# Elementwise work of GpSimd moved to VectorE in the opening of a three-stage kernel (one core)

## The chip, the cores and the metric

The kernel runs on one core of one Trainium2 chip. The metric is device time in microseconds (us) of one execution. A core has TensorE (PE in the profile, with its weight loads as PEld), VectorE (DVE), ScalarE (ACT), GpSimd (POOL) and SyncE (SP, which here only issues DMAs). Each engine works through its own queue in order and waits on semaphores of the others.

## The reference, cut to what matters

Three layers follow each other. The first is gated linear attention over 4 batches, 8 heads, 768 positions and head size 48; the second a dense layer with the Mish activation; the third a top-1 mixture of eight experts.

```
for t in range(S):                                  # attention
    state = alpha[t][:, None] * state + outer(k[t], v[t])
    y[t] = q[t] @ state
h = x @ w_in;  g = h * tanh(softplus(h));  x2 = g @ w_out          # 3072 x 384 -> 2048 -> 384
expert = argmax(x2 @ w_gate);  out = gate * relu(x2 @ w1[expert]) @ w2[expert]
```

## The kernel before, in words

Tokens go in 8 tiles of 384; a tile is 3 attention units of 128 positions of one batch (24 units, all 8 heads in each). A tile takes 16 steps, one for each 128 columns of the hidden layer. A step is `mm1` (9 matmuls, L622), the activation (`act_tanh` for each step, `act_mish` for three steps at once) and, six steps later, `mm2` (9 matmuls, L680). After the 16th `mm2` of a tile, `route` picks the expert. Matrices are split into a high half, which ScalarE writes by rounding, and a low half, the difference: three products stand for one full one.

Before the steady loop over tiles there is an opening, whose order is a string of short tokens: attention of units 0 to 5 (`a_prep1`, `a_prep2`, `a_kt`, `a_qk`, `a_y`, `a_kv`), the unpacking of 16 weight blocks (`prep_w`, then `prep_c` for the gate's columns), and the steps 0 to 15 of the first tile as their weights arrive. The compiler's scheduler puts each engine's instructions in order by its own estimate of when each is ready, so the order in a queue is not that of the string.

What the change touches:

- `prep_w(f)`: ScalarE makes the exponent part (L61), VectorE assembles the words in four instructions (L62, L63, L66, L69), ScalarE writes the high halves of w_in and w_out (L408), GpSimd the two low halves (L409). Two blocks of words (`wbits`) and two raw blocks (`wraw`) are held; the next raw block's DMA waits for L69.
- `a_prep1(u)`: two scans on VectorE (L437, L451) of alpha against reset rows `rst1`, `rst2`, with small instructions between (L444, L447, L448).
- `a_prep2(u)`: products of k (L463, GpSimd) and q (L464, VectorE for units 0 to 2, else GpSimd) with the scans.
- `a_qk(u)`: the masked scores. For units 0 to 5 ScalarE copies them out of PSUM (L506) and GpSimd masks them (L507); for later units VectorE does both in one instruction (L512).
- `act_mish(s)`: VectorE multiplies (L665), ScalarE rounds to the high half (L666), GpSimd subtracts for the low half `gl` (L668).

Of the kernel before, what the change touches and what calls it, by code (L numbers as in the profile page):

```python
# [7 lines left out]
F32 = mybir.dt.float32  # L8
# [4 lines left out]
AF = mybir.ActivationFunctionType  # L13
ALU = mybir.AluOpType
# [4 lines left out]
P = 128  # L19
B, H, S, D = 4, 8, 768, 48  # L20
NP = H // 2
NCH = S // P
NU = B * NCH
NT, DM = B * S, H * D
DFF = 2048
NF = DFF // P
# [5 lines left out]
NTILE = NT // TT  # L32
G = TT // P
# [23 lines left out]
def w_bits(nc, t, raw):  # L57
    words = raw.bitcast(I32).rearrange("p (n t) -> p n t", t=2)
    hi, lo = words[:, :, 1], words[:, :, 0]
    tf = t.bitcast(F32)  # L60
    nc.scalar.activation(out=tf, in_=hi.bitcast(F32), func=AF.Abs)  # L61
    nc.vector.tensor_scalar(out=tf, in0=tf, scalar1=MINW, scalar2=None, op0=ALU.max)  # L62
    nc.vector.tensor_scalar(  # L63
        out=t, in0=t, scalar1=3, scalar2=0x3FFFFFFF, op0=ALU.logical_shift_left, op1=ALU.bitwise_and
    )
    nc.vector.scalar_tensor_tensor(  # L66
        out=t, in0=hi, scalar=-0x40000000, in1=t, op0=ALU.bitwise_and, op1=ALU.bitwise_or
    )
    nc.vector.scalar_tensor_tensor(  # L69
        out=t, in0=lo, scalar=29, in1=t, op0=ALU.logical_shift_right, op1=ALU.bitwise_or  # L70
    )
# [203 lines left out]
def kernel(ctx: ExitStack, tc: tile.TileContext, att, w_io, w_gate, w1, w2, out):  # L275
    nc = tc.nc
    root = ctx.enter_context(ExitStack())

    const = root.enter_context(tc.tile_pool(name="const", bufs=1))
# [26 lines left out]
    def wt_f(f):  # L306
        return [t[:, f % (NF // 2)] for t in wt[f // (NF // 2)]]
# [13 lines left out]
    def bank(u, name):  # L321
        if u < G:
            nps[0] += 1
            k = nps[0] % 5
            if k < 2:
                return ps_a.tile([P, 512], F32, tag="att", name=name)
            return ps_acc.tile([P, 512], F32, tag=f"acc{k - 2}", name=name)
        return ps_a.tile([P, 512], F32, tag="att", name=name)
# [12 lines left out]
    def load_w(f):  # L341
        if f < NF:
            wraw[f] = s0p.tile([P, 2 * DM], I64, tag="wraw", name="wraw", bufs=2)
            nc.sync.dma_start(out=wraw[f], in_=w_io[f])
# [6 lines left out]
    load_unit(2)  # L351
    load_w(1)

    ident = const.tile([P, P], F32, name="ident")
    nc.gpsimd.memset(ident, 1.0)
    nc.gpsimd.affine_select(
        out=ident, in_=ident, pattern=[[-1, P]], compare_op=ALU.is_equal, fill=0.0, base=0, channel_multiplier=1
    )
    mask = const.tile([P, P], F32, name="mask")
    nc.gpsimd.memset(mask, 1.0)  # L360
    nc.gpsimd.affine_select(
        out=mask, in_=mask, pattern=[[1, P]], compare_op=ALU.is_ge, fill=0.0, base=0, channel_multiplier=-1
# [4 lines left out]
        out=before, in_=before, pattern=[[1, P]], compare_op=ALU.is_gt, fill=0.0, base=0, channel_multiplier=-1  # L367
# [12 lines left out]
    for e in range(E):  # L380
        nc.gpsimd.memset(ecap[:, e:e + 1], e * ROOM / P)
        nc.gpsimd.memset(full[:, :, e:e + 1], float((e + 1) * ROOM))
        nc.gpsimd.memset(desc[:, :, e:e + 1], float(E - e))
    rst1 = const.tile([P, NP, P + 1], F32, name="rst1")
    rst2 = const.tile([P, NP, P + 1], F32, name="rst2")
    nc.gpsimd.memset(rst1, 0.0)
    nc.gpsimd.memset(rst1[:, :, 0:1], 1.0)
    nc.gpsimd.memset(rst2, 0.0)
    chk = const.tile([P, NTILE * G * E + NU * NP], F32, name="chk")
    chk_l = chk[:, 0:NTILE * G * E].rearrange("p (j g e) -> p j g e", g=G, e=E)  # L390
    chk_a = chk[:, NTILE * G * E:].rearrange("p (u a o) -> p u a o", a=NP, o=1)
# [8 lines left out]
    def prep_w(f):  # L400
        raw = wraw.pop(f)
        t = s0p.tile([P, 2 * DM], I32, tag="wbits", name="wbits", bufs=2)
        tf = t.bitcast(F32)
        w_bits(nc, t, raw)
        ih, il, oh, ol = wt_f(f)
        ih, il = (x.rearrange("p k m -> p (k m)") for x in (ih, il))
        for h, l, x in ((ih, il, tf[:, 0:DM]), (oh, ol, tf[:, DM:])):
            nc.scalar.activation(out=h[:, 0:DM], in_=x, func=AF.Copy)  # L408
            nc.gpsimd.tensor_tensor(out=l[:, 0:DM], in0=x, in1=h[:, 0:DM].bitcast(F32), op=ALU.subtract)  # L409
        load_w(f + 2)  # L410
        wb[f] = tf

# [43 lines left out]
    def a_prep2(u):  # L456
        if u >= NU:
            return
        t = unit_t[u]
        sc1, sc2 = st[u]  # L460
        q3 = t[:, OQ:OK].rearrange("p (a b) -> p a b", b=P)
        k3 = t[:, OK:OV].rearrange("p (a b) -> p a b", b=P)
        nc.gpsimd.tensor_tensor(out=k3, in0=k3, in1=sc1[:, :, 1:], op=ALU.mult)  # L463
        (nc.vector if u < G else nc.gpsimd).tensor_tensor(out=q3, in0=q3, in1=sc2[:, :, 1:], op=ALU.mult)  # L464
        st[u] = [sc1, k3, q3]

    state = {}
# [21 lines left out]
    def a_qk(u):  # L489
        sc1, kc, qc, kn, am = st[u]  # L490
        both = [bank(u, "qk").rearrange("p (a b) -> p a b", b=P) for _ in range(2)]
        last = None
        for a in range(NP):
            for i in (1, 0):
                r = slice(64 * i, 64 * i + 64)
                mm = nc.tensor.matmul(both[i][:, a], kc[r, a], qc[r, a], start=True, stop=True)
                if last is not None:
                    tc.add_manual_dep(
                        mm.ins, last.ins.name,
                        mybir.DependencyInfo(mybir.DependencyClass.NoSync, mybir.DependencyReason.DATA),  # L500
                        reason="heads in turn"
                    )
                last = mm
        for i in (1, 0):
            if u < 2 * G:
                nc.scalar.activation(out=am[:, :, i], in_=both[i], func=AF.Copy)  # L506
                nc.gpsimd.affine_select(  # L507
                    out=am[:, :, i], in_=am[:, :, i], pattern=[[0, NP], [1, P]], compare_op=ALU.is_ge, fill=0.0,
                    base=0, channel_multiplier=-1
                )  # L510
            else:
                nc.vector.tensor_tensor(  # L512
                    out=am[:, :, i], in0=both[i], in1=mask.unsqueeze(1).to_broadcast([P, NP, P]), op=ALU.mult
                )

    def a_y(u):
        sc1, kc, qc, kn, am = st[u]
# [47 lines left out]
    def att_phase(u, k):  # L565
        if u >= NU:
            return
        if k == 0:
            a_kt(u)
        elif k == 1:  # L570
            a_qk(u)
            a_prep1(u + 1)
        elif k == 2:
            pass
        elif k == 3:
            a_y(u)
            a_prep2(u + 1)
        else:
            a_kv(u)
            load_unit(u + 2)  # L580
# [47 lines left out]
    def after_act(inst):  # L628
        for x in inst:
            if seq:  # L630
                tc.add_manual_dep(
                    x.ins, seq[0].ins.name,
                    mybir.DependencyInfo(mybir.DependencyClass.NoSync, mybir.DependencyReason.DATA), reason="tables"
                )
            seq[:] = [x]
# [15 lines left out]
    def act_mish(s):  # L651
        b, i = divmod(s, KB)
        if i < KB - 1 and s < NTILE * NF - 1:
            return
        h, t = batch.pop(b)
        tf = t[:, 0:i + 1].rearrange("p k t -> p (k t)")
        after_act([
            nc.scalar.activation(out=tf, in_=tf, func=AF.Arctan, scale=-0.5, bias=half),
            nc.scalar.preload_act_table_set("silu_and_others"),
            nc.scalar.activation(out=tf, in_=tf, func=AF.Sin, scale=-2.0, bias=quart),  # L660
        ])
        for x in range(i + 1):
            gh = s2p.tile([P, TT], F32R, tag="gh", name="gh", bufs=KB)
            gl = s2p.tile([P, TT], F32R, tag="gl", name="gl", bufs=KB)
            nc.vector.tensor_tensor(out=t[:, x], in0=t[:, x], in1=h[:, x], op=ALU.mult)  # L665
            nc.scalar.activation(out=gh, in_=t[:, x], func=AF.Copy)  # L666
            eng = nc.vector if s == NTILE * NF - 1 else nc.gpsimd
            eng.tensor_tensor(out=gl, in0=t[:, x], in1=gh.bitcast(F32), op=ALU.subtract)  # L668
            live[s - i + x] = (gh, gl)

# [14 lines left out]
    fill = []  # L685
# [78 lines left out]
    def step(s):  # L764
        if s < nsteps:
            mm1(s)
            act_tanh(s)
            act_mish(s)
        d = s - LAG
        if d >= 0:  # L770
            mm2(d)
            if d % NF == NF - 1:
                return route(d // NF)
# [10 lines left out]
    def more_w(_):  # L784
# [3 lines left out]
    nsteps = NTILE * NF  # L788
    does = {
        "a": a_prep1, "b": a_prep2, "t": a_kt, "q": a_qk, "y": a_y,  # L790
        "v": a_kv, "l": load_unit, "w": prep_w, "c": prep_c, "h": warm, "m": step, "z": zero, "P": more_w
    }
    warm(12)
# [8 lines left out]
    for s in range(NF, nsteps + LAG):  # L802
# [17 lines left out]
        out=flb, in0=fl[:, 0:1], scalar1=0.0, scalar2=0.0, op0=ALU.is_le, op1=ALU.is_equal  # L820
# [11 lines left out]
        out=flag, in0=fl[:, 1:2], scalar=float(CAP), in1=fl[:, 2:3], op0=ALU.is_gt, op1=ALU.add  # L832
# [218 lines left out]
```

## Time and profile before

| what | value |
| --- | --- |
| time, median of 3 runs | 901.82 us (900.13 to 905.32) |
| profiled execution, its own time | 900.5 us |
| its span in the profile | 898.8 us |
| busy: PE, DVE, ACT, POOL | 827.8, 501.4, 525.3, 321.8 us |
| mean granted TensorE clock | 0.957 |

The span is what lies between the first and the last instruction; 1.7 us of the execution lie outside it. Busy time is a union of intervals, waits for a busy port included; a line of the `lines` view adds the idle time of the engine just before the group, and what ended it.

### The profile page before, as it was taken

What the parts mean: (1) busy time and instruction counts of PE and PEld (TensorE: products, weight loads), DVE (VectorE), ACT (ScalarE), POOL (GpSimd) and SP (SyncE); (2) the same over time, 40 slices, a digit from 0 to 9 for tenths busy, and PEclk for the clock granted to TensorE, in tenths of its full rate; (3) what the DMA queues carried; (4) which work ended last, traced back from release to release, by engine and by line L of the source; (5) the groups of instructions that cost most, each with busy time, mean ns of one, the idle gap of its engine ahead of it and who ended that gap; (6) DMA issues with size and microseconds to landing.
All of it is one profiled execution on the core that took longest, in us unless ns stands there. A gap on an engine that the chain in (4) does not pass through costs nothing. (4 is left out here: it accounts for less than half of the span.)

```text
span 898.8 us, 15088 instructions
## 1 busy us (share of the span) xinstructions
PE 827.8 (92%) x5988; PEld 761.1 (85%) x5988; DVE 501.4 (56%) x952; ACT 525.3 (58%) x826; POOL 321.8 (36%) x359
## 2 busy tenths in 40 slices
PE   7778785999999999999999999996699999999994
PEld 4667675889999999999999989896699999999994
DVE  7986876476465676566566554734443553354220
ACT  3365665657776677766776667884443653455221
POOL 5674754254344444354354342243001011100111
PEclk9787797999999999999999999999799999999998
DMA  6733342721022012112121101300733543453001
GB/s 245 237 106 118 106 133 100 207 80 65 29 86 76 15 69 91 40 48 83 45 77 48 49 27 48 95 28 19 238 120 126 177 150 106 147 182 116 26 30 34
DMA packets 22012, 85.86 MB, mean 96 GB/s; under 512 B 3232, under 2 KB 9012, under 8 KB 18988
## 3 DMA queue, kind: packets, MB, share of 16 engines
q1 hardware_dynamic: 18348, 75.31, 25.7%
q0 software_dynamic: 3584, 9.50, 3.0%
q8 instruction: 49, 0.80, 0.4%
q14 instruction: 31, 0.25, 0.1%
HBM read 68.35 MB, written 17.03 MB: 95 GB/s over the span
## 5 line engine op out<-in xcount | busy, mean ns | idle before, releaser
L668 POOL TENSOR_TENSOR gl<-tau,gh 128x384 fp32r<-128x384 f32 x126 | 135.0, 1081 | 171.7 <-ACT gh L666 116.8
L622 PE MATMUL h<-xh,wi_h 128*128 128x384 f32 x384 | 138.0, 360 | 8.7 <-ACT wi_h L408 6.1
L622 PE MATMUL h<-xh,wi_l 128*128 128x384 f32 x384 | 134.2, 350 | 5.1 <-POOL wi_l L409 5.0
L680 PE MATMUL acc<-wo_h,gh 128*128 128x392 f32 x384 | 133.4, 348 | 1.6 <-ACT gh L666 1.0
L622 PE MATMUL h<-xl,wi_h 128*128 128x384 f32 x384 | 133.3, 347 | 0.0
L680 PE MATMUL acc<-wo_l,gh 128*128 128x392 f32 x384 | 132.4, 345 | 0.0
L665 DVE TENSOR_TENSOR tau<-tau,hc 128x384 f32<-128x384 f32 x128 | 81.6, 690 | 86.1 <-ACT tau L660 46.0
L680 PE MATMUL acc<-wo_h,gl 128*128 128x392 f32 x384 | 126.5, 346 | 1.5 <-POOL gl L668 1.5
L888 PE MATMUL g<-eh,ew 128*128 128x432 f32 x384 | 118.6, 363 | 0.0
L648 ACT ACTIVATE tau<-h 128x384 f32<-128x384 f32 x128 | 60.7, 490 | 91.5 <-PE h L622 64.4
L902 POOL DMA_INDIRECT out_dram<-yo,xg x32 | 31.7, 991 | 228.8 <-ACT yo L901 214.2
L933 PE MATMUL y<-hh,ew 128*128 128x432 f32 x336 | 105.5, 365 | 1.4 <-ACT hh L892 1.4
L893 DVE SCALAR_TENSOR_TENSOR hl<-g,hh 128x432 fp32r<-128x432 f32 x64 | 38.5, 603 | 91.4 <-ACT hh L892 91.4
L666 ACT ACTIVATE gh<-tau 128x384 fp32r<-128x384 f32 x128 | 66.0, 523 | 37.7 <-PE acc L680 19.3
L622 PEld LDWEIGHTS h<-xh,wi_h 128*128 128x128 f32 x384 | 74.2, 194 | 15.5 <-ACT wi_h L408 8.2
L609 DVE TENSOR_TENSOR ew<-est,ew 128x512 fp32r<-128x512 f32 x96 | 64.2, 718 | 34.7 <-ACT ew L608 33.3
L892 ACT ACTIVATE hh<-g 128x432 fp32r<-128x432 f32 x64 | 33.4, 524 | 82.4 <-PE g L888 82.0
L622 PEld LDWEIGHTS h<-xh,wi_l 128*128 128x128 f32 x384 | 74.6, 194 | 8.1 <-POOL wi_l L409 7.2
L649 DVE COPY hc<-h 128x384 f32<-128x384 f32 x128 | 67.9, 545 | 19.1 <-ACT tau L648 19.1
L680 PEld LDWEIGHTS acc<-wo_h,gh 128*128 128x128 f32 x384 | 73.4, 191 | 3.5 <-ACT gh L666 2.2
L888 PEld LDWEIGHTS g<-eh,ew 128*128 128x128 f32 x384 | 72.7, 190 | 3.4
L622 PEld LDWEIGHTS h<-xl,wi_h 128*128 128x128 f32 x384 | 74.4, 194 | 1.1 <-issue 0.6
(141 smaller groups left out, 1621.7 us busy)
## 6 DMA issues: line engine op xcount, KB each, us to landing
unit<-in_att_dram SPq DMA_DIRECT2D x23, 1026.5 KB
est<-in_w_dram SPq DMA_DIRECT2D x28, 768.0 KB
wraw<-in_w_io_dram SPq DMA_DIRECT2D x16, 768.0 KB
xs<-zrow SPq DMA_DIRECT2D x3, 1746.0 KB
xg<-xs SPq DMA_DIRECT2D x7, 654.8 KB
est<-in_w_dram SPq DMA_DIRECT2D x4, 512.0 KB
xs<-zrow SPq DMA_DIRECT2D x1, 1552.0 KB
est<-in_w_dram SPq DMA_DIRECT2D x4, 256.0 KB
```

The costliest lines, as they stand in the source:

```text
L609: nc.vector.tensor_tensor(out=tl[:, cs], in0=tx, in1=th[:, cs].bitcast(F32), op=ALU.subtract)
L622: nc.tensor.matmul(ps, l[:, k], r[:, k], start=(n == 0), stop=(n == 3 * KC - 1))
L648: nc.scalar.activation(out=t[:, i], in_=hbuf[s], func=AF.Tanh, scale=0.5)
L649: nc.vector.tensor_copy(out=h[:, i], in_=hbuf.pop(s))
L665: nc.vector.tensor_tensor(out=t[:, x], in0=t[:, x], in1=h[:, x], op=ALU.mult)
L666: nc.scalar.activation(out=gh, in_=t[:, x], func=AF.Copy)
L668: eng.tensor_tensor(out=gl, in0=t[:, x], in1=gh.bitcast(F32), op=ALU.subtract)
L680: nc.tensor.matmul(acc[j][g][:, 0:DM + E], l[:, gs], w, start=(f == 0 and i == 0), stop=(f == NF - 1 and i == 2))
L888: nc.tensor.matmul(ps, l[:, k, fs], r[:, k], start=(n == 0), stop=(n == 3 * KC - 1))
L892: nc.scalar.activation(out=hh, in_=ps, func=AF.Relu)
L893: nc.vector.scalar_tensor_tensor(out=hl, in0=ps, scalar=0.0, in1=hh.bitcast(F32), op0=ALU.max, op1=ALU.subtract)
L933: nc.tensor.matmul(yac[e][c], l[:, f, cs], r, start=(f == 0 and i == 0), stop=(f == NF2 - 1 and i == 2))
```

## The change

Four kinds of GpSimd work go to VectorE, and the reset rows are set before the other constants. The low halves of all 16 weight blocks, the k and q products of units 0 to 5, the low halves of the steps that are activated before step 16 (`s < NF`, five batches of three) and the masks of units 0 to 5 are VectorE's; the masks read PSUM directly, and ScalarE's copy in front of them goes. Left on GpSimd are the constants, the check L441, the state product L484, and the products of units from 6 on.

```diff
@@ (constants)
+    rst1 = const.tile([P, NP, P + 1], F32, name="rst1")
+    rst2 = const.tile([P, NP, P + 1], F32, name="rst2")
+    nc.gpsimd.memset(rst1, 0.0)
+    nc.gpsimd.memset(rst1[:, :, 0:1], 1.0)
+    nc.gpsimd.memset(rst2, 0.0)
     ident = const.tile([P, P], F32, name="ident")
...
-    (the same five lines, behind the other constants)
@@ prep_w
-            nc.gpsimd.tensor_tensor(out=l[:, 0:DM], in0=x, in1=h[:, 0:DM].bitcast(F32), op=ALU.subtract)
+            nc.vector.tensor_tensor(out=l[:, 0:DM], in0=x, in1=h[:, 0:DM].bitcast(F32), op=ALU.subtract)
@@ a_prep2
-        nc.gpsimd.tensor_tensor(out=k3, in0=k3, in1=sc1[:, :, 1:], op=ALU.mult)
-        (nc.vector if u < G else nc.gpsimd).tensor_tensor(out=q3, in0=q3, in1=sc2[:, :, 1:], op=ALU.mult)
+        eng = nc.vector if u < 2 * G else nc.gpsimd
+        eng.tensor_tensor(out=k3, in0=k3, in1=sc1[:, :, 1:], op=ALU.mult)
+        eng.tensor_tensor(out=q3, in0=q3, in1=sc2[:, :, 1:], op=ALU.mult)
@@ a_qk
-            if u < 2 * G:
-                nc.scalar.activation(out=am[:, :, i], in_=both[i], func=AF.Copy)
-                nc.gpsimd.affine_select(out=am[:, :, i], in_=am[:, :, i], ...)
-            else:
-                nc.vector.tensor_tensor(out=am[:, :, i], in0=both[i], in1=mask..., op=ALU.mult)
+            nc.vector.tensor_tensor(out=am[:, :, i], in0=both[i], in1=mask..., op=ALU.mult)
@@ act_mish
-            eng = nc.vector if s == NTILE * NF - 1 else nc.gpsimd
+            eng = nc.vector if s < NF or s == NTILE * NF - 1 else nc.gpsimd
```

## Rows read from the trace of the kernel before

**Rows 1.** Busy time by stretch: span, PE, PEld, DVE, ACT, POOL, clock, DMA.
```profile
0.00:165.00 165.00, 126.33 (x916) 106.66 (x917) 122.06 (x162) 87.49 (x157) 95.09 (x124) 0.82 0.46 154
165.00:190.00 25.00, 23.70 (x212) 21.58 (x211) 16.90 (x48) 18.91 (x28) 8.12 (x10) 1.00 0.49 151
10.00:60.00 50.00, 38.35 (x328) 31.27 (x328) 45.34 (x60) 25.96 (x49) 34.62 (x31) 0.80 0.54 180
```

**Rows 2.** Waits of PE, 0 to 165 us: total, times, longest.
```profile
PE wc L423 <- ACT wot L420: 11.8, 5, 4.3
...
PE h L622 <- POOL wi_l L409: 5.0, 5, 2.7
...
PE y L534 <- POOL am L507: 1.0, 1, 1.0
```

**Rows 3.** Groups of POOL by line, 0 to 172 us: busy, mean ns, idle before.
```profile
L409 POOL TENSOR_TENSOR wo_l<-wbits,wo_h 128x384 fp32r<-128x384 f32 x16 | 22.9, 1429 | 0.0
L668 POOL TENSOR_TENSOR gl<-tau,gh 128x384 fp32r<-128x384 f32 x16 | 20.9, 1325 | 9.5 <-ACT gh L666 7.0 <-issue 2.5
L409 POOL TENSOR_TENSOR wi_l<-wbits,wi_h 128x384 fp32r<-128x384 f32 x16 | 19.3, 1206 | 40.3 <-ACT wi_h L408 37.5 <-PE wt L418 2.9
L463 POOL TENSOR_TENSOR unit<-unit,sc 128x512 f32<-128x512 f32 x8 | 10.8, 1355 | 0.6
L507 POOL TENSOR_SCALAR_AFFINE_SELECT am<-am 128x512 f32<-128x512 f32 x12 | 9.0, 765 | 1.2 <-ACT am L506 1.2
```

**Rows 4.** Groups of DVE by line, 0 to 172 us.
```profile
L66 DVE SCALAR_TENSOR_TENSOR wbits<-wraw,wbits 128x768 int32<-128x768 int32 x16 | 19.1, 1195 | 0.3
L69 DVE SCALAR_TENSOR_TENSOR wbits<-wraw,wbits 128x768 int32<-128x768 int32 x16 | 16.9, 1059 | 0.2
L62 DVE TENSOR_SCALAR wbits<-wbits 128x768 f32<-128x768 f32 x16 | 15.3, 956 | 14.0 <-ACT wbits L61 14.0
L63 DVE TENSOR_SCALAR wbits<-wbits 128x768 int32<-128x768 int32 x16 | 14.0, 878 | 0.4
L665 DVE TENSOR_TENSOR tau<-tau,hc 128x384 f32<-128x384 f32 x18 | 13.2, 782 | 5.2 <-ACT tau L660 5.2
...
L448 DVE SCALAR_TENSOR_TENSOR rst<-sc,rc 128x4 f32<-128x4 f32 x8 | 6.9, 865 | 0.2
```

**Rows 5.** Timeline of DVE: start us, us, instruction.
```profile
6.36 1.16 DVE L448 SCALAR_TENSOR_TENSOR rst<-sc,rc 128x4 f32<-128x4 f32 x1
...
34.07 0.15 DVE L448 SCALAR_TENSOR_TENSOR rst<-sc,rc 128x4 f32<-128x4 f32 x1
...
96.95 0.96 DVE L66 SCALAR_TENSOR_TENSOR wbits<-wraw,wbits 128x768 int32<-128x768 int32 x1
...
100.48 0.56 DVE L62 TENSOR_SCALAR wbits<-wbits 128x768 f32<-128x768 f32 x1 [1.00 <-ACT wbits L61]
```

**Rows 6.** Timeline of POOL, same columns.
```profile
4.54 0.10 POOL L387 MEMSET rst<- 128x4 f32 x1
...
6.31 1.19 POOL L463 TENSOR_TENSOR unit<-unit,sc 128x512 f32<-128x512 f32 x1
...
46.63 1.93 POOL L409 TENSOR_TENSOR wo_l<-wbits,wo_h 128x384 fp32r<-128x384 f32 x1
...
104.76 4.70 POOL L668 TENSOR_TENSOR gl<-tau,gh 128x384 fp32r<-128x384 f32 x3
...
155.61 2.91 POOL L668 TENSOR_TENSOR gl<-tau,gh 128x384 fp32r<-128x384 f32 x3
```

**Rows 7.** Line L668 alone, whole span: duration min/median/max in ns.
```profile
L668 POOL TENSOR_TENSOR gl<-tau,gh x126: 988/1020/1729, 54.3 to 615.9; 128x384 fp32r<-128x384 f32 x126
...
L668 DVE TENSOR_TENSOR gl<-tau,gh x2: 544/550/557, 617.3 to 618.0; 128x384 fp32r<-128x384 f32 x2
```

**Rows 8.** Mask of later units on DVE, groups by line, 0 to 260 us.
```profile
L512 DVE TENSOR_TENSOR am<-qk,mask 128x512 f32<-128x512 f32 x8 | 5.2, 679 | 1.3 <-PE qk L496 1.3
```

**Rows 9.** PE's first instructions, timeline, columns as in rows 5.
```profile
1.90 7.69 PE L760 MATMUL warm<-ones 128*128 128x512 bf16 x28 [1.90 <-POOL ones L374]
```

More of the change, by code (lines that the diff above doesn't have):

```diff
@@ L383 @@
         nc.gpsimd.memset(desc[:, :, e:e + 1], float(E - e))
[L384 to L388, printed above, removed]
     chk = const.tile([P, NTILE * G * E + NU * NP], F32, name="chk")
@@ L504, in a_qk @@
         for i in (1, 0):
-            if u < 2 * G:
-                nc.scalar.activation(out=am[:, :, i], in_=both[i], func=AF.Copy)
[L507 to L510, printed above, removed]
-            else:
-                nc.vector.tensor_tensor(
-                    out=am[:, :, i], in0=both[i], in1=mask.unsqueeze(1).to_broadcast([P, NP, P]), op=ALU.mult
-                )
+            nc.vector.tensor_tensor(
+                out=am[:, :, i], in0=both[i], in1=mask.unsqueeze(1).to_broadcast([P, NP, P]), op=ALU.mult
+            )
     def a_y(u):
```

## The prediction

> **What bounds the kernel now.** I first read busy time by stretch. From 0 to 165 us PE works 126.3 of 165 us and its clock is granted at 0.82 on the mean, so it swings between its two levels, 1.2 and 2.4 GHz; from 165 to 190 us it works 23.7 of 25 us at 1.00 [rows 1]. Behind 190 us PE stays the bound, and the change has no instruction there (its units are 0 to 5, its steps those below 16). So everything is decided in the opening: a microsecond by which PE fills up earlier is a microsecond of the whole.
>
> In the opening no engine is full. DVE works 122.1 us, ACT 87.5, POOL 95.1 [rows 1]; DVE's gaps are 42.9 us, and in the densest stretch, 10 to 60 us, it is busy 45.3 of 50 us, a share of 0.907 [rows 1]. Then I read whom PE waits for: ACT's copy for the gate columns 11.8 us, POOL's low half of w_in 5.0, POOL's masks 1.0 [rows 2].
>
> Last I read the durations, and they carry the argument. L448 works on four columns. It takes 1.16 us beside POOL's k product of 1.19 us and 0.15 us by itself [rows 5, 6]. L62 takes 0.56 us at its shortest and 0.956 on the mean [rows 4, 5]. On the other side, `gl` on POOL has a median of 1.02 us, but three of them beside a busy DVE take 4.70, that is 1.57 each [rows 6, 7]. The two engines hold each other up, in both directions. Much of DVE's 122 and POOL's 95 us is standing at a shared door.
>
> **The change, part by part.** All sums are made against the profiled execution's own 900.5 us (span 898.8 and 1.7 outside it); the median of the runs, 901.8, is 1.3 above.
>
> *What goes from POOL and comes to DVE.* Moved are 32 low halves of weights, 15 low halves of steps (five batches of three), nine 512-wide products (six of k, three of q) and twelve masks. On POOL they take 22.9 + 19.3 = 42.2 us, 15 x 1.325 = 19.9, 9 x 1.355 = 12.2 and 12 x 0.765 = 9.2 [rows 3], 83.5 us in all. On DVE a 384-wide subtraction takes 0.55 us [rows 7], and a 512-wide product with one operand in PSUM 0.68 [rows 8], which I take for both operands in SBUF too: 47 x 0.55 + 9 x 0.68 + 12 x 0.68 = 25.9 + 6.1 + 8.2 = 40.2 us.
>
> *What DVE gets back.* Mean less shortest, times the count: L62 16 x (0.956 - 0.56) = 6.3; L63, also single-source over 768 columns and so put at 0.56, 16 x 0.32 = 5.1; L66 16 x (1.195 - 0.96) = 3.8; L69 at the same 0.96 1.6; L665 at 0.55 18 x 0.23 = 4.2; L448 8 x (0.865 - 0.15) = 5.7 [rows 4, 5, 7]. That is 26.7 us. DVE's work is then 122.1 - 26.7 + 40.2 = 135.6 us: 13.5 us more on the engine that is already the busiest of the three, with 83.5 us less on POOL. The sign is not plain from this, so I price the pieces where they lie.
>
> *384-wide subtractions.* Where POOL does one while DVE stands, it is on the path by itself. Going through both timelines, I count 15 such pieces over 0.3 us, from a part of the `wo_l` at 46.63 to the last of the three `gl` from 155.61 [rows 6], 11.5 us together, 11.3 instructions' worth. Each saves 1.02 - 0.55 = 0.47 us: -5.3. The other 36 run beside DVE. There one POOL instruction and one DVE instruction of 0.96 us together take 1.57 us [rows 5, 6]; behind each other on DVE they take 0.96 + 0.55 = 1.51. That saves 0.06 us each: -2.2.
>
> *Products.* With k on POOL the unit's next small instruction L448 waits for it, about 1.15 us in five of the six units; then 0.15 + 0.68 = 0.83 on DVE: 5 x -0.32 = -1.6. The q of units 3 to 5 I put at nothing (at 0.68 against POOL's mean of 1.36 it can be -2.0; if DVE is needed elsewhere, +2.0).
>
> *Masks.* DVE gets 8.2 us. POOL's work on them lies for 2.3 us (four pieces) beside an idle DVE, which goes; the other nine instructions' worth shared DVE's door. In the pair above 1.02 + 0.96 - 1.57 = 0.41 us run side by side, so 0.765 - 0.41 = 0.36 of each is serial: 3.2. Net 8.2 - 2.3 - 3.2 = +2.7. PE's wait of 1.0 for a mask goes [rows 2]: -1.0. ACT loses twelve copies; I put this at nothing, with PE's 11.8 us of waits for an ACT copy [rows 2] as the end of what it could give.
>
> *Reset rows first.* The last of them is set at 4.54 to 4.64 us and the first scan starts right then [rows 6]. Set earlier, that wait may shrink, at the least by nothing if alpha's own DMA lands no sooner. Against that `ones` comes later by the three memsets, and PE's 28 warming matmuls wait for it and then hold PE until 9.6 us [rows 9]. Each of the two effects I bound by 1.2 us, and take nothing.
>
> Sum: -5.3 - 2.2 - 1.6 + 2.7 - 1.0 = -7.4 us; I add -1.3 for the raw blocks' loop (their DMA and ACT's next L61 follow L69 and the low halves, and DVE waits 14.0 us for L61 [rows 4]; a tenth of it). That is -8.7: 891.8 for the profiled execution, 893.1 beside the median. What is late next is ACT's chain from L69 to the copy that PE waits for.
>
> No DMA is issued in another order, and none is passed on SP's queue; the raw loads only come earlier with L69. What the change adds is waits of DVE on ACT: for both low halves and for `gl` it must now wait for ACT's rounding, with all of its later work queued behind. POOL spent 37.5 us idle for that same high half [rows 3], which cost little there.
>
> What the Trainium skill says weighs on both sides. The page "SBUF — State Buffer", section "Who interferes with whom", has the pair of ports between the two engines as a lock held for a whole instruction. The 1.16 us of L448 agree; the pair of 1.57 us does not quite, since 0.41 us overlap. By the rule's letter a pair would cost 0.96 + 1.02 = 1.98 now, each of the 36 would save 0.47, and the sum would be -23.4, or 877. Against the change speaks "Perfetto Trace Analysis", section "Optimizing Scalar/DVE Operations": moving work between these two engines might not help, because they share a port. By that rule the rival of the full DVE queue, below, is the case; no row so far bears it out for the whole opening.
>
> **The rivals.**
>
> *DVE runs dense.* The gaps close as far as in the best stretch. Then 135.6 / 0.907 = 149.5 us for the opening, 15.5 earlier: about 886, with up to 8 more if PE's clock stays up. For it: POOL's work is no longer late in its own queue. Against: gaps of DVE that wait for ACT stay.
>
> *DVE becomes the queue for everything (slower).* An instruction on DVE that waits for ACT's rounding stops all that lies behind, weights, scans and evacuations of PSUM that PE waits for. At the share of before, 122.1 / 165 = 0.74, the opening takes 135.6 / 0.74 = 183 us, 18 later: 920. The point that decides: DVE's gaps are 42.9 us now; if more than 165 - 135.6 = 29.4 us of them stay, the kernel is slower. For it: POOL's idle 37.5 us behind ACT [rows 3]. Against: POOL had little else to do then, while DVE has.
>
> *Hidden.* ACT's in-order chain sets PE's pace (11.8 us [rows 2]), POOL and DVE are both beside it, and the moved work vanishes in gaps: 901.
>
> **How the numbers follow.** My forecast, 893 with its own range of 885 to 899, has 0.42; dense 0.20; the DVE queue 0.21; hidden 0.17. Less than 0.5% (4.5 us) cannot be told from no change; that puts the border at 897.3. Faster: 0.39 of the forecast's 0.42 and all of dense, 0.59. Same: 0.03 and most of hidden, 0.18. Slower: the DVE queue and the rest, 0.23. For eight in ten I go from 877 (dense, clock kept) to 911, half of the way into the DVE queue.
>
> **What would show it.** Right: L62, L63, L66, L69, L448 and L665 near their shortest; POOL's busy time to 165 us near 95 - 84 = 11; DVE busy near 135 us with fewer than 29 us of gaps; the first tile's `route`, and all behind it, some 9 us earlier. Wrong: DVE idle in front of the low halves with ACT as the releaser, or DVE's durations still long with POOL idle. An unchanged DVE share with PE's waits for L420 still there would mean the hidden case.

## The result, and the profile after

The changed kernel takes 890.65 us (median of four runs, 889.86 to 891.61) beside 900.98 for the kernel before in the same session (899.18 to 905.32): ratio 0.9879, interval 0.9847 to 0.9911, 10.3 us less. The profiled execution took 891.61 us, its span is 889.7.

The page of the changed kernel, engine totals and two of its rows in 40 slices:

```profile
PE 824.2 (93%) x5988; PEld 760.6 (85%) x5988; DVE 503.9 (57%) x1020; ACT 520.3 (58%) x814; POOL 242.7 (27%) x291
...
DVE  7988794765665677565665644743543553355220
...
POOL 2100020354354355354354342252001101100111
```

POOL is nearly empty in the first seven slices, those of the opening; all told it lost 79 us of work and DVE gained 2.5. Busy time by stretch, columns as in [rows 1]:

```profile
0.00:165.00 165.00, 131.83 (x976) 114.56 (x978) 131.08 (x242) 90.17 (x157) 19.21 (x61) 0.84 0.50 170
...
0.00:60.00 60.00, 44.03 (x358) 32.96 (x359) 52.52 (x96) 24.77 (x44) 8.11 (x50) 0.89 0.58 207
60.00:110.00 50.00, 41.73 (x268) 38.63 (x268) 39.26 (x75) 30.76 (x56) 0.94 (x1) 0.80 0.33 116
110.00:165.00 55.00, 46.07 (x363) 42.97 (x353) 39.31 (x73) 34.63 (x59) 10.16 (x10) 0.84 0.56 178
```

The same stretches of the kernel before:

```profile
0.00:60.00 60.00, 46.45 (x359) 34.85 (x360) 50.49 (x66) 27.25 (x50) 40.12 (x77) 0.83 0.58 198
60.00:110.00 50.00, 38.05 (x226) 34.48 (x225) 37.81 (x51) 30.27 (x54) 27.30 (x24) 0.80 0.36 121
110.00:165.00 55.00, 41.83 (x335) 37.33 (x334) 33.76 (x47) 29.97 (x53) 27.67 (x25) 0.84 0.43 136
```

Read the matmul counts: by 60 us PE has done as many as before (358; 359 before), from 60 to 110 us it does 268 (226 before), from 110 to 165 us 363 (335). The lead is made where weight blocks and steps of the first tile fill the queues, not in the attention units at the start. Routing, the last work of each tile, shows that it is kept. All 24 calls of `ecap` by line, the kernel before and then the changed one (min/median/max in ns, first and last start in us):

```profile
L717 PE MATMUL rank<-ecap,ones x24: 166/166/180, 186.1 to 622.8; 128*128 128x8 bf16 x24
...
L711 PE MATMUL rank<-ecap,ones x24: 166/166/180, 176.1 to 612.4; 128*128 128x8 bf16 x24
```

The first is 10.0 and the last 10.4 us earlier now. From the last to the end of the span it is 277.3 us, 276.0 before. So all of the gain lies ahead of 176 us, and the last `route` is a mark by which the experiments' openings can be compared without their third stage.

DVE's groups, 0 to 172 us, as in [rows 4]; then POOL's one group of `gl`:

```profile
L66 DVE SCALAR_TENSOR_TENSOR wbits<-wraw,wbits 128x768 int32<-128x768 int32 x16 | 15.6, 974 | 0.2
L69 DVE SCALAR_TENSOR_TENSOR wbits<-wraw,wbits 128x768 int32<-128x768 int32 x16 | 15.2, 949 | 0.1
...
L659 DVE TENSOR_TENSOR tau<-tau,hc 128x384 f32<-128x384 f32 x21 | 10.5, 554 | 8.0 <-ACT tau L654 7.9
...
L409 DVE TENSOR_TENSOR wi_l<-wbits,wi_h 128x384 fp32r<-128x384 f32 x16 | 9.6, 597 | 1.6 <-ACT wi_h L408 1.6
L63 DVE TENSOR_SCALAR wbits<-wbits 128x768 int32<-128x768 int32 x16 | 9.2, 573 | 0.2
L506 DVE TENSOR_TENSOR am<-qk,mask 128x512 f32<-128x512 f32 x14 | 9.0, 679 | 0.0
L62 DVE TENSOR_SCALAR wbits<-wbits 128x768 f32<-128x768 f32 x16 | 8.8, 550 | 8.4 <-ACT wbits L61 8.4
L409 DVE TENSOR_TENSOR wo_l<-wbits,wo_h 128x384 fp32r<-128x384 f32 x16 | 8.8, 548 | 0.0
L662 DVE TENSOR_TENSOR gl<-tau,gh 128x384 fp32r<-128x384 f32 x15 | 7.7, 549 | 0.0
```

```profile
L662 POOL TENSOR_TENSOR gl<-tau,gh 128x384 fp32r<-128x384 f32 x4 | 3.9, 1006 | 7.6 <-ACT gh L660 7.6
```

The old forms are near their shortest: L62 956 to 550 ns, L63 878 to 573, the product of `act_mish` (L659, was L665) 782 to 554. The low halves took 1206 to 1429 ns on POOL and take 548 to 597 on DVE. PE's waits to 165 us, as in [rows 2]:

```profile
PE wc L423 <- ACT wot L420: 9.0, 5, 4.0
PE h L616 <- ACT wi_h L408: 4.1, 3, 3.0
PE kv L551 <- DVE am L506: 3.4, 2, 3.1
```

The 5.0 us for POOL's low half are gone. In their place stand 3.4 us for the masks, now in DVE's queue (1.0 for POOL's before).

### The profile page after: what moved, and what is told of

It is laid out like the page before. It is cut to its first block, busy times and chain, and to the rows that moved or that the text cites. A ratio compares the mean times of both kernels' runs of the same rounds, so it can differ in the third digit from the quotient of the medians.

```text
span 889.7 us, 15049 instructions
## 1 busy us (share of the span) xinstructions
PE 824.2 (93%) x5988; PEld 760.6 (85%) x5988; DVE 503.9 (57%) x1020; ACT 520.3 (58%) x814; POOL 242.7 (27%) x291
## 5 line engine op out<-in xcount | busy, mean ns | idle before, releaser
L662 POOL TENSOR_TENSOR gl<-tau,gh 128x384 fp32r<-128x384 f32 x111 | 114.7, 1041 | 163.7 <-ACT gh L660 110.2
L659 DVE TENSOR_TENSOR tau<-tau,hc 128x384 f32<-128x384 f32 x128 | 75.3, 642 | 89.3 <-ACT tau L654 63.9
L927 PE MATMUL y<-hh,ew 128*128 128x432 f32 x336 | 105.4, 365 | 1.9 <-ACT hh L886 1.9
```

What stands on the lines that cost most here:

```text
L927: nc.tensor.matmul(yac[e][c], l[:, f, cs], r, start=(f == 0 and i == 0), stop=(f == NF2 - 1 and i == 2))
```

## The experiments

The theory: in the opening POOL's and VectorE's elementwise instructions, which read SBUF, stretch each other, and the change took that away. Rivals: VectorE's queue was relieved by a piece alone (masks off ACT and POOL), the earlier reset rows did it, or any POOL work, reading or not, costs the same. Each ratio is against the kernel before, run beside it. "Last `route`" is the mark above, from one profiled execution, which took up to 3.1 us more than its kernel's median (masks alone, 907.9); the last column is what lies behind it to the end of the span.

| kernel | median us | ratio (interval) | last `route` | behind |
| --- | --- | --- | --- | --- |
| before (in the first four's runs) | 900.97 | 1 | 622.8 | 276.0 |
| changed | 890.65 | 0.9879 (0.9847 to 0.9911) | 612.4 | 277.3 |
| weights alone | 894.53 | 0.9922 (0.9903 to 0.9942) | 615.7 | 277.0 |
| masks alone | 904.80 | 1.0054 (1.0033 to 1.0075) | 628.8 | 277.4 |
| products alone | 897.74 | 0.9963 (0.9949 to 0.9977) | 620.3 | 276.5 |
| `gl` alone | 895.62 | 0.9939 (0.9923 to 0.9955) | 619.0 | 276.7 |
| changed, masks back | 891.54 | 0.9877 (0.9848 to 0.9906) | 614.3 | 275.9 |
| changed, reset rows late | 899.78 | 0.9977 (0.9958 to 0.9996) | 617.3 | 281.9 |
| changed, 47 POOL reads added | 907.57 | 1.0059 (1.0039 to 1.0078) | 630.1 | 276.6 |
| changed, 47 POOL memsets added | 890.24 | 0.9872 (0.9837 to 0.9907) | 611.9 | 276.9 |
| changed, reset rows behind `ones` | 888.67 | 0.9856 (0.9835 to 0.9877) | 611.6 | 277.2 |
| changed, reset rows behind `mask` | 892.88 | 0.9898 (0.9879 to 0.9917) | 614.5 | 277.2 |
| changed, `hc` copied by ACT | 889.69 | 0.9869 (0.9849 to 0.9890) | 615.2 | 275.1 |
| reset rows late, masks first | 893.11 | 0.9902 (0.9884 to 0.9920) | 614.4 | 277.5 |

### One part at a time

Each of these four is the kernel before with one hunk of the change. Weights:

```diff
-            nc.gpsimd.tensor_tensor(out=l[:, 0:DM], ..., op=ALU.subtract)
+            nc.vector.tensor_tensor(out=l[:, 0:DM], ..., op=ALU.subtract)
```

> The kernel before with one part of the change: the 32 low halves of weights on VectorE. Theory A (the two engines hold each other up at a shared port, and VectorE does the same subtraction in about half the time): two thirds of the moved 384-wide work, so about two thirds of its term: 4 to 7 us faster than before, 894 to 897; L62, L63, L66 and L69 near 0.56, 0.56, 0.96 and 0.96 us except beside gl and the products. Theory B (what counts is only how soon a result reaches TensorE, one engine less in the chain): PE's waits for the low half go, 5.0 us at the most, and VectorE's other durations matter nothing: 0 to 3 us faster. Theory C (VectorE becomes the queue): 2 to 8 us slower.

Masks (the hunk of `a_qk`):

```diff
-            if u < 2 * G:
...
+            nc.vector.tensor_tensor(out=am[:, :, i], in0=both[i], in1=mask..., op=ALU.mult)
```

> The kernel before with one part of the change: the twelve masks of units 0 to 5 on VectorE out of PSUM, without ScalarE's copy. Theory A: 8.2 us more for VectorE against little lock time given back: 0 to 4 us slower, 901 to 905. Theory B (shorter chain of a unit, one instruction for two on two engines, about 0.9 us per unit, and ScalarE relieved of 7 us): 2 to 5 us faster, 896 to 899. Theory C: 4 to 10 us slower.

Products:

```diff
+        eng = nc.vector if u < 2 * G else nc.gpsimd
+        eng.tensor_tensor(out=k3, ...)
+        eng.tensor_tensor(out=q3, ...)
```

> The kernel before with one part of the change: the k products of units 0 to 5 and the q products of units 3 to 5 on VectorE. Theory A: L448 falls from about 1.1 to 0.15 us in these units, 0 to 3 us faster, 898 to 901. Theory B: the unit's first transposes wait for k, which comes no sooner: within 1 us of before. Theory C: 2 to 5 us slower.

Low halves of the steps:

```diff
-            eng = nc.vector if s == NTILE * NF - 1 else nc.gpsimd
+            eng = nc.vector if s < NF or s == NTILE * NF - 1 else nc.gpsimd
```

> The kernel before with one part of the change: the 15 low halves of the first steps on VectorE. Theory A: a third of the 384-wide work: 1 to 4 us faster, 897 to 900. Theory B: the second matmuls come six steps later and wait for nothing here: within 1 us of before. Theory C (VectorE stands waiting for ScalarE's rounding): 1 to 5 us slower.

Measured: -6.4, +3.8, -3.2 and -5.3 us. Weights and masks came inside the ranges of theory A; the products and the low halves of the steps gained 0.3 and 1.4 us more than it allowed. Alone, the subtractions gain most. The masks alone lose, and the trace has the rival that was to be slower, in small. PE's waits to 165 us with the masks alone on DVE, then one DVE group of it:

```profile
PE qk L496 <- DVE wo_l L425: 6.7, 2, 3.7
PE kv L550 <- DVE s L553: 4.6, 1, 4.6
...
PE wt L418 <- DVE wbits L69: 4.1, 1, 4.1
```

```profile
L658 DVE TENSOR_TENSOR tau<-tau,hc 128x384 f32<-128x384 f32 x15 | 14.7, 1030 | 1.9 <-ACT tau L653 1.9
```

DVE took more work while POOL still stretched this form (1030 ns; 782 before), and PE stands behind DVE's queue: the three waits were 4.9, 0.4 and 0 us before.

The four differences add up to -11.1 us. The changed kernel's -10.3 is not what to hold beside them, for it has the early reset rows too. The four parts together without those are the kernel "reset rows late" of the table: 899.78 us, only 1.9 less than the kernel before beside it (901.65). By the last `route` the four add up to -7.1 + 6.0 - 2.5 - 3.8 = -7.4; together they gave -5.5, and 5.9 us were lost behind that mark (281.9; 276.0 before). Each edit lets the scheduler order all queues anew, so a single part's 3 us hold its order as well as its cost.

### POOL's reads against POOL's writes

The test that holds the order fixed. To the changed kernel 47 POOL instructions are added, beside the 47 low halves that were moved. One kernel's read a high half twice:

```diff
+            nc.gpsimd.tensor_tensor(out=junk, in0=h[:, 0:DM].bitcast(F32), in1=h[:, 0:DM].bitcast(F32), op=ALU.subtract)
...
+            if s < NF:
+                nc.gpsimd.tensor_tensor(out=junk, in0=gh.bitcast(F32), in1=gh.bitcast(F32), op=ALU.subtract)
```

> The changed kernel, and GpSimd does the 47 subtractions of 384 columns besides, on the same high halves and into a scratch row that nobody reads. Nothing of the changed kernel waits for them. Theory A (they hold VectorE up at the shared port): VectorE's busy time to 165 us grows by 10 to 25 us by longer instructions, L62 and L66 go back to about 0.9 and 1.2 us, and the kernel loses 5 to 15 us, 896 to 906. Theory B (only the wait for GpSimd's results counted): within 1.5 us of the changed kernel.

The other's only write, behind the same ACT instructions:

```diff
+            after(nc.gpsimd.memset(junk, 0.0), [hi])
...
+            if s < NF:
+                after(nc.gpsimd.memset(junk, 0.0), [hi])
```

> The changed kernel, and GpSimd writes zeros into 776 scratch columns, 47 times, each after the same ScalarE instruction; GpSimd reads nothing. Theory A with a lock for every instruction of GpSimd: as with the dummy subtractions, 896 to 906, all six of VectorE's two-operand and single-operand forms longer. Theory A with a lock on reads alone for two-operand instructions: L66, L69 and L665's successor stay at 0.96, 0.96 and 0.55 us, only L62 and L63 grow, and the kernel loses 0 to 5 us. Theory B: within 1.5 us of the changed kernel.

Nothing uses what they write. In both traces the instructions of DVE, ACT and PE stand in the changed kernel's order throughout the opening. With the reads, DVE's groups to 172 us, then POOL's:

```profile
L410 DVE TENSOR_TENSOR wo_l<-wbits,wo_h 128x384 fp32r<-128x384 f32 x16 | 14.5, 904 | 0.0
L410 DVE TENSOR_TENSOR wi_l<-wbits,wi_h 128x384 fp32r<-128x384 f32 x16 | 14.0, 877 | 1.6 <-ACT wi_h L409 1.6
L664 DVE TENSOR_TENSOR gl<-tau,gh 128x384 fp32r<-128x384 f32 x15 | 11.5, 799 | 0.0
L62 DVE TENSOR_SCALAR wbits<-wbits 128x768 f32<-128x768 f32 x16 | 11.0, 690 | 5.8 <-ACT wbits L61 5.8
```

```profile
L411 POOL TENSOR_TENSOR zrow<-wi_h 128x384 f32<-128x384 f32 x16 | 17.2, 1075 | 61.6 <-ACT wi_h L409 61.4
```

One pair by timeline, DVE and then POOL (start, duration):

```profile
112.62 1.18 DVE L410 TENSOR_TENSOR wi_l<-wbits,wi_h 128x384 fp32r<-128x384 f32 x1
...
116.36 0.56 DVE L410 TENSOR_TENSOR wi_l<-wbits,wi_h 128x384 fp32r<-128x384 f32 x1 [0.59 <-ACT wi_h L409]
```

```profile
111.94 1.45 POOL L411 TENSOR_TENSOR zrow<-wi_h 128x384 f32<-128x384 f32 x1 [2.52 <-ACT wi_h L409]
...
116.47 1.14 POOL L411 TENSOR_TENSOR zrow<-wi_h 128x384 f32<-128x384 f32 x1 [1.98 <-ACT wi_h L409]
```

The same subtraction takes 1.18 us where POOL's had begun 0.68 us ahead of it, and 0.56 us where it began 0.11 us ahead of POOL's. So it is with DVE's 47 low halves: 16 met none of POOL's two-input instructions and took 0.53 to 0.55 us, 5 began ahead of one and took 0.55 to 0.56, and the 23 that began with 0.7 us or more of one to go took 1.12 to 1.30 (three met only its last 0.25 us).

The kernel takes 907.57 us, 16.9 more than the changed one: 0.36 us for each POOL instruction, though nobody waits for any of them. DVE is busy 143.1 us to 165 (131.1), as theory A had it, but the time is 1.6 us past its range, and L62 and L66 came to 0.69 and 1.02 us, not to 0.9 and 1.2. Most of the growth lies in the low halves, which wait for the same ACT instructions as POOL's reads. With the memsets, the same views:

```profile
L410 DVE TENSOR_TENSOR wi_l<-wbits,wi_h 128x384 fp32r<-128x384 f32 x16 | 9.7, 608 | 1.8 <-ACT wi_h L409 1.8
L62 DVE TENSOR_SCALAR wbits<-wbits 128x768 f32<-128x768 f32 x16 | 9.6, 602 | 7.6 <-ACT wbits L61 7.6
```

```profile
L411 POOL MEMSET zrow<- 128x776 f32 x32 | 24.6, 768 | 57.9 <-ACT wi_h L409 56.9
L666 POOL MEMSET zrow<- 128x776 f32 x15 | 11.8, 786 | 20.7 <-ACT gh L662 20.0
```

The memsets take 36.4 us of POOL (the reads 49.5), and the time is 890.24. L66 and L69, with two inputs, stay at 950 and 949 ns; of the 16 L62, with one, four took 0.65 to 0.99 us. With the order held, it is POOL's reads that hold DVE up, and hardly its writes.

### Masks back, and the copy of `hc` on ACT

The masks' hunk undone in the changed kernel:

```diff
+            if u < 2 * G:
+                nc.scalar.activation(out=am[:, :, i], in_=both[i], func=AF.Copy)
+                nc.gpsimd.affine_select(out=am[:, :, i], in_=am[:, :, i], ...)
```

> The changed kernel with the masks of units 0 to 5 put back on ScalarE and GpSimd. Theory A (shared port; the parts add up): the masks alone cost 3.8 us, so this comes out 2 to 6 us under the changed kernel, 885 to 889, and beats both. Theory B (with the other parts moved VectorE and GpSimd no longer collide, so that masks there cost nothing, and what they give to ScalarE counts): 890 to 894, no better than the changed kernel.

891.54 us: no gain, so my theory of the masks' price fell in this company. DVE is busy 127.54 us to 165 (131.08), and PE waits 12.2 us for `wot` (9.0): ACT's twelve copies are back in the queue that PE waits for. The order of the queues differs here too, so the price of the masks by themselves stays open.

```diff
+        if s < NF:
+            nc.scalar.activation(out=h[:, i], in_=hs, func=AF.Copy)
```

> The changed kernel with the copy of the hidden layer out of PSUM on ScalarE for the first 16 steps, 0.49 us there for 0.55 on VectorE. Theory A as far as it goes on (VectorE, 131 of 165 us busy, is the fullest engine of the opening, ScalarE 90): 2 to 6 us faster than the changed kernel, 884 to 889. Rival (TensorE waits for ScalarE's queue, its copy for the gate columns above all): 1 to 6 us slower, 892 to 897.

Neither. 889.69 us cannot be told from the changed kernel. DVE has 4.7 us less work, but PE's waits for `wot` are 11.4 and for `wi_h` 6.4 us (9.0 and 4.1): what DVE got, ACT's chain took.

### The reset rows

```diff
-    (rst1, rst2 and their three memsets, in front of `ident`)
+    (the same, behind the loop that fills `ecap`, `full` and `desc`)
```

> The changed kernel with the reset rows set where they were before, behind the other constants. Theory A (the first scan waits for alpha's own transfer, and TensorE's warming matmuls for the constants, and VectorE is full behind both): within 1.5 us of the changed kernel, 889 to 892. Rival (the earlier first scan is worth its whole wait): 1.5 to 3 us slower than the changed kernel, 892 to 894.

899.78 us: most of the gain gone, and slower than either expectation. The traces split it. Last `route` is at 617.3, 4.9 us behind the changed kernel's; the rest lies past it, 281.9 us to the end against 277.3. There PE's order differs: a transpose (L862) stands ahead of the matmuls of L927 and waits for VectorE, and behind the two waits the matmuls take 0.56 us again, 0.36 only from about 647 us on (granted clock 0.51 from 640 to 647 us, 1.00 from there to 660). PE's timeline there:

```profile
640.44 0.98 PE L862 MATMUL t<-ident,xg 108*128 108x108 f32 x4 [2.44 <-DVE el L866]
643.07 1.45 PE L927 MATMUL y<-hh,ew 128*128 128x432 f32 x3 [1.65 <-ACT hh L886]
644.32 0.56 PE L927 MATMUL y<-hl,ew 128*128 128x432 f32 x1
```

In the opening, timeline of this kernel, DVE and then PE:

```profile
4.68 1.23 DVE L437 TENSOR_TENSOR_SCAN sc<-unit,rst 128x516 f32<-128x516 f32 x1 [4.68 <-POOL rst L387]
...
32.29 1.23 DVE L437 TENSOR_TENSOR_SCAN sc<-unit,rst 128x516 f32<-128x516 f32 x1 [1.00 <-DMA unit<-in_att_dram]
...
33.49 1.28 DVE L506 TENSOR_TENSOR am<-qk,mask 128x512 f32<-128x512 f32 x2
```

```profile
34.33 1.12 PE L551 MATMUL kv<-unit,kn 128*64 128x64 f32 x16 [5.87 <-DVE am L506]
...
37.92 1.01 PE L616 MATMUL h<-xh,wi_h 128*128 128x384 f32 x2
```

The scan at 32.29 us waits 1.00 us for its DMA, the masks stand behind it in DVE's queue, and PE waits 5.87 us for them. In the changed kernel, the same places:

```profile
4.27 1.23 DVE L437 TENSOR_TENSOR_SCAN sc<-unit,rst 128x516 f32<-128x516 f32 x1 [4.27 <-DMA unit<-in_att_dram]
```

```profile
30.91 1.12 PE L551 MATMUL kv<-unit,kn 128*64 128x64 f32 x16 [3.13 <-DVE am L506]
...
34.52 1.01 PE L616 MATMUL h<-xh,wi_h 128*128 128x384 f32 x2
```

The first scan is 0.41 us later and the first step 3.4 us. Is it the time of the rows, or the order that the scheduler makes of it? Two more places for the same five lines, behind `ones` and `ids`, and behind `ident` and `mask`:

```diff
     nc.gpsimd.iota(ids, ...)
+    (rst1, rst2 and their three memsets)
     ecap = const.tile([P, E], BF16, name="ecap")
```

> The changed kernel with the reset rows set a little later: behind the constants up to the token numbers, in front of the expert tables, so about 1.6 us later than in the changed kernel but before alpha has landed. The scheduler's order on ScalarE is that of the changed kernel, and on VectorE and TensorE nearly (0.90 and 0.98 of it). Theory D (what the late reset rows cost is the order that the scheduler makes of 0.4 us, not the 0.4 us): 888 to 893, as the changed kernel. Rival E (the time at which the rows are set counts): slower than the changed kernel by 2 to 6 us.

```diff
+    (rst1, rst2 and their three memsets)
     before = const.tile([P, P], BF16, name="before")
```

> The changed kernel with the reset rows set behind the identity and the mask, some 0.5 us later than in the changed kernel and long before alpha has landed. The scheduler's order is a third one (0.68 of VectorE's, 0.76 of TensorE's order as in the changed kernel). Theory D: the time is that of another order, anywhere from 886 to 900, and over 3 us from the changed kernel. Rival E: within 1.5 us of the changed kernel, since the first scan starts when alpha lands in both.

888.67 and 892.88 us. With the rows behind `ones` the first scan starts at 4.48 us, half of the way to 4.68, and nothing is lost. Of DVE's instructions to 172 us, 250 of 251 there stand in the changed kernel's sequence, 173 of 247 in the late one (counted in the traces, gaps allowed). The second place has a third order (186 of 247); it is 2.2 us off the changed kernel and fits neither expectation. But its first scan starts at 4.44 us, no later than behind `ones`, and the kernel takes 4.2 us more: it is not the start of the scan that counts. Last, the late kernel with the masks of unit 2 put ahead of the scans of units 3 and 4:

```diff
+        if u in (3, 4):
+            tc.add_manual_dep(scan.ins, masks[2].ins.name, ...)   # order only, same engine
```

> The kernel with late reset rows (899.8), and in VectorE's queue the first scans of units 3 and 4 are put behind the masks of unit 2, by an order without a wait. With late reset rows alone the scheduler has these masks behind both scans, and the second scan waits for its unit's transfer, while TensorE waits 5.9 us for a mask. Theory D (what the late rows cost is that an instruction which waits for a transfer stands in front of one that TensorE needs, in one in-order queue): TensorE's long wait for the mask shrinks under 3.5 us, the first step starts 2 to 4 us earlier, near 35 us, and the kernel regains 3 to 9 us: 890 to 897. Rival (the loss is spread over an order that is worse in many places, of which this is one): the wait goes, and the time stays within 2 us of 899.8.

893.11 us, 6.7 won back with the rows still late. PE in this kernel:

```profile
29.55 1.12 PE L557 MATMUL kv<-unit,kn 128*64 128x64 f32 x16 [0.93 <-DVE am L512]
...
33.15 1.01 PE L622 MATMUL h<-xh,wi_h 128*128 128x384 f32 x2
...
37.81 0.69 PE L622 MATMUL h<-xl,wi_h 128*128 128x384 f32 x1 [3.65 <-DVE xl L543]
```

The wait for the mask is 0.93 instead of 5.87 us and the first step starts 4.8 us earlier, more than expected; a new wait of 3.65 takes part of it back, and the last `route` comes 2.9 us earlier. Of the 7.3 us between the two spans the other 4.4 lie in the third stage, whose order this edit moved too. So another order wins back most of what the late rows cost; that the masks behind that one scan are all of it isn't shown.

No kernel here beats the changed one beyond doubt: 888.67 us (ratio 0.9856, 0.9835 to 0.9877) overlaps its interval.

## Why the prediction was right, and where it was off

*Sign, place and size.* 893 was forecast, with 885 to 899 as the forecast's own range; 890.65 came. The first `route` was to be some 9 us earlier and is 10.0. That the size came out is luck in part. The sum of -8.7 is made of the four moved parts, with the reset rows at nothing; the kernel with just these four parts gained 1.9 us, 5.5 by the last `route`. With the rows still late, another order brought it to 893.11. So the moved work can give what was forecast, but how much of it shows hangs on the order of the queues, for which the sum has no term.

*What DVE gets back:* right nearly to the number. Mean before less mean after, times the count before: L62 6.5, L63 4.9, L66 3.5, L69 1.8, the product 4.1, L448 (158 ns now) 5.7, together 26.5 us; 26.7 were put down. The moved work takes 26.1 us for the subtractions (25.9 forecast) and 679 to 726 ns for masks and products (680). That DVE is busy 131.1 and not 135.6 us, although more work falls into the same 165 us (21 products of `act_mish`, 18 before), is in how busy time is counted. It is a union, and queued instructions overlap; DVE's timeline of the changed kernel:

```profile
99.94 0.96 DVE L66 SCALAR_TENSOR_TENSOR wbits<-wraw,wbits 128x768 int32<-128x768 int32 x1
100.81 0.55 DVE L409 TENSOR_TENSOR wi_l<-wbits,wi_h 128x384 fp32r<-128x384 f32 x1
101.28 0.55 DVE L409 TENSOR_TENSOR wo_l<-wbits,wo_h 128x384 fp32r<-128x384 f32 x1
```

Each begins 0.08 or 0.09 us ahead of the end of the one before it. Added up, DVE's durations to 165 us rose from 129.1 to 146.1 us, the union from 122.1 to 131.1.

The Trainium skill, page "SBUF — State Buffer", section "Who interferes with whom", makes the shared pair of ports a lock for a whole instruction. The 0.56 and 1.18 us above agree roughly for reads. The same section excepts a GpSimd instruction that only writes, where VectorE's has two inputs in SBUF; L66 and L69 beside the memsets (950 and 949 ns) agree. The estimate of 877 by the lock's letter did not come: 890.65.

*The subtractions:* the term was mis-sized, and nothing here gives its true size. It was -7.5 (15 beside an idle DVE, 36 beside a busy one at 0.06 each); the two parts alone gave -6.4 and -5.3, or -7.1 and -3.8 by the last `route`, while all four parts together gave -5.5 by that mark. Its 0.06 compares unlike things: 1.57 us for the pair is from start to start (4.70 us for three), 1.51 a sum of durations. From start to start the pair on DVE takes 0.87 + 0.47 = 1.34 us in the rows above, so by this estimate each of the 36 saves 0.23 and all of them 8 us instead of 2.2. The four parts gave less than the sum would be with that; whether DVE's time is not worth its full length everywhere, or the order of the queues took some back, stays open. What the result of a subtraction costs those who wait for it was left out: on POOL a low half took 1.2 to 1.4 us behind ACT's rounding, on DVE 0.55 to 0.60, and PE's 5.0 us of waits for it went. How much of the gain is that latency and how much DVE's shorter forms was not taken apart; the added reads (0.36 us each, with nobody waiting for POOL) show only that the second is real.

*Products:* -1.6 forecast, -3.2 alone, though L448 fell only to 546 ns there and not to 150. The q of units 3 to 5, put at nothing with an end at -2.0, can be the rest; so can the order.

*Masks:* +1.7 forecast; +3.8 alone, but next to nothing (-0.9) when all the rest is in. The net was right in sign where POOL still stretches DVE. ACT's copies, put at nothing, may count: PE's 9.0 us for `wot` are 12.2 when they come back.

*Reset rows:* the step that failed. "Take nothing", each effect bounded by 1.2 us, and in this company they are worth 9.1 us (4.9 by the last `route`). The bound was right for the two effects it named: the first scan is 0.4 us earlier, and `ones` lets PE's warming begin at 2.49 instead of 1.90 us, with its end where it was. What it missed is that a small shift lets the scheduler choose another order for in-order queues. That term could not have been read from the trace of before.

*The rivals.* "DVE becomes the queue for everything" was to decide at 29.4 us of gaps: 165 - 131.1 = 33.9 stay, and the kernel is faster. The point was wrong: it took the opening's work as fixed within 165 us and 135.6 as DVE's part of it, by sums and not by the union. Its mechanism is real, though: the masks alone and PE's waits of 3.13 us (changed) and 5.87 us (rows late) for a mask show it. "Hidden" holds for ACT's copy of `wot`, still PE's longest wait at 9.0 us. "Dense" did not come: DVE's share from 10 to 60 us rose to 47.7 of 50, but from 60 to 165 us it is 0.75. The 8 us that this case added for PE's clock had no row behind them; the granted clock to 165 us is 0.84 (0.82 before). The page "Perfetto Trace Analysis" of the Trainium skill, section "Optimizing Scalar/DVE Operations", says that offloading between these two engines might not help. Here it did, at 0.9879, and the four moved parts without the early rows hardly did, at 0.9977.

*POOL,* forecast at 11 us to 165, is at 19.2: unit 7 and the first `gl` of the second tile now begin before 165 us, and what stayed on POOL can take longer beside the fuller DVE (unit 6's product of k 2.82 us, 1.17 before).

## What to carry to other kernels

Where GpSimd and VectorE both read SBUF and VectorE is the busier, price a GpSimd instruction twice: its own time on the path, and what it adds to VectorE's (here 0.36 us of the kernel's time for 384 columns). Constants and memsets may stay on GpSimd. Take a change apart down to the hunk that looks harmless: here three memsets at another place decided whether the rest was worth 1.9 us or 10.3. A difference of one part below one per cent is an effect only when the order in the queues is the same in both kernels; compare the orders first, or add work that leaves them alone.

## What was not expected of the hardware

POOL's memsets of 776 columns, 36.4 us of them, cost nothing measurable, although L62 went from 550 to 602 ns on the mean. The 612 ns of `gl` there (549) are one instruction of 1.54 us beside a product on POOL, which reads; its median is 548. And beside a read the one that starts first keeps its time: 0.55 to 0.56 us for the five low halves that began ahead of POOL's, while POOL's then took 1.0 to 1.2.
